# Level two of the first and fifth gate/up products inside PSUM, first pair of a pass plain, last pair between the first down products

## The chip, the cores and the metric

The kernel runs on one core of one Trainium2 chip. Time is device microseconds (us) of one execution. Where two kernels are compared, they ran on the same chip in the same rounds. "Ratio" is the mean time of one kernel's fast runs over the mean of the other's fast runs of the same rounds, so it is not quite the ratio of the medians that are quoted beside it.

## The reference, cut to what matters

```python
# x: 2048 tokens x 1024; w_gate, w_up: 1024 x 3584; w_down: 3584 x 1024
x = x + A(layernorm(x), wqkv, wo)               # linear attention, 32 heads
x = x + B(layernorm(x), w_gate, w_up, w_down)
x = x + A(layernorm(x), wqkv, wo)
x = x + B(layernorm(x), w_gate, w_up, w_down)

def B(x):
    h = (x @ w_gate) * (x @ w_up)               # no nonlinearity
    return h @ w_down
```

## The kernel before

Each layer B is done in two passes of 1024 tokens. A pass has a gate/up stage, in 14 "pairs", and a down stage. A pair is one block of gate columns (A) and the same block of up columns (B). Both stages use a Strassen scheme in Winograd's form: seven products `1` to `7` of half-size blocks instead of eight, with sums of weight blocks and of token blocks made beforehand by VectorE. One product of a pair is 4 matmuls of 512 columns for A and 4 for B.

Some of these products are split a second time ("level two"): gate and up blocks together form a 2 x 2 block product, which becomes seven small products of 2 matmuls with 256 columns each. That is 14 x 256 columns in place of 8 x 512, an eighth less TensorE work. Its price is small sums of tokens and weights, and the assembly of the results. Before, the partial results go from PSUM to SBUF by ScalarE and VectorE and are added in when the product is finished. The orders of work in a pair are strings. `P1A` is product 1 for the gate block, `D2B` finishes product 2 for the up block, and `26` is step 6 of level two of product 2. A prime means that the step belongs to the pair before, `S2+` loads or makes weight sums for the next pair, `R` loads the next weights into a ring of five slots, `T0` and `T1` are places for other work.

```python
L2SETS = {(False, 0): "", (False, 1): "24", (True, 0): "234", (True, 1): "234"}
ORDER0 = "P1A P5A P6A D2A P7A D3B' P1B D4A T0 P6B R0 D3A P7B R1 P5B D4B D2B T1"
ORDER1 = "T0 P1A D3B' 21 P1B 26 P6A 27 P6B S3= D2A 41 D2B P5A 46 P7A 47 P7B D4A P5B R D3A D4B S2+ T1"
ORDER2 = "21 P1A P1B D3A' D3B' 26 S3= P6A T0 27 D2A 41 P6B D2B 46 P7A 31 47 S2+ P7B D4A 36 D4B P5A P5B 37 T1 R"
# first pass: ORDER0; second pass: ORDER1; third and fourth: ORDER2

def st6():                                   # level two, one of its steps
    mm(5, yk, 0, True)
    acp(c5, rc5, yk)                         # ScalarE, PSUM to SBUF
    mm(6, xk, 0, False)
    acp(ss[:, 1], rss[1], xk)
    tt(ss[:, 1], ss[:, 1], c5, ALU.add, ...) # VectorE, in SBUF
# ... cut ...
# last steps of the second layer A: output tiles of 128 tokens, i = 0..15
    y_grp(tok[i], 0, i); y_seed(i + 1); nxt.b2_one(); y_grp(tok[i], 1, i)
    if not first and i == 12:
        for k in range(5):
            stash(3 + k)                     # x tiles to DRAM: their room is wanted
# ... cut ...
def ticks0(u):                               # called at T0 (u even) and T1 (u odd)
    if u % 4 < 2 and not lnp.done():
        lnp.flush_step()                     # one LayerNorm step
    if first and u:
        wd_tick(u)                           # T0: load w_down block, T1: its sums
```

Of the kernel before, what the change touches and what calls it, by code (L numbers as in the profile page):

```python
# [180 lines left out]
def build_kernel(nc, A_x, A_wqkv, A_wo, B_w_gate, B_w_up, B_w_down, out):  # L181
# [5 lines left out]
    SG = 4.0  # L187
# [13 lines left out]
    L2SETS = {(False, 0): "", (False, 1): "24", (True, 0): "234", (True, 1): "234"}  # L201
    ORDER0 = "P1A P5A P6A D2A P7A D3B' P1B D4A T0 P6B R0 D3A P7B R1 P5B D4B D2B T1"
    ORDER1 = "T0 P1A D3B' 21 P1B 26 P6A 27 P6B S3= D2A 41 D2B P5A 46 P7A 47 P7B D4A P5B R D3A D4B S2+ T1"
    ORDER2 = "21 P1A P1B D3A' D3B' 26 S3= P6A T0 27 D2A 41 P6B D2B 46 P7A 31 47 S2+ P7B D4A 36 D4B P5A P5B 37 T1 R"
# [59 lines left out]
    O_TP = {"3": RE, "2": RE + 3072, "4": RB + 28672}  # L264
    O_CP = O_R
    O_SS = [None, O_R + 8192]
    O_C5 = [O_R + 14336, O_R + 15360]
# [25 lines left out]
    KSP = {(q, i): dkey("sp%s%d" % (q, i)) for q in "23" for i in range(2)}  # L293
    KSPW = {(q, i): dkey("spw%s%d" % (q, i)) for q in "23" for i in range(2)}
# [14 lines left out]
    spscr = nc.dram_tensor("sp_scratch", (NJ, 128, 3072), F16, kind="Internal").ap()  # L309
# [5 lines left out]
    with ExitStack() as es:  # L315
# [72 lines left out]
        B_DX = [5, 6, 7, 4]  # L388
# [308 lines left out]
        DPROD = ["1", "2", "7", "4", "6", "5", "3"]  # L697
# [4 lines left out]
        def sp_place(ps_, p, q):  # L702
            sz, so = (2048, 0) if q == "2" else (1024, 2048)
            xp = O_X + (8 * ps_ + 3) * D * 2
            o = {"2": (xp + 4096, RC), "3": (O_R + 12288, xp + 8192)}[q][p % 2]
            return sz, so, o, R(V_SP + 64 * p + so // 64, 32)
# [69 lines left out]

        def tp_ops(pair, prods):
            s0 = pair * 1024
            res = []
            for q in prods:  # L780
                if q == "4":
                    x, base, st_ = T4, O_T + 8192, 1024
                else:
                    s1 = s0 + (512 if q == "3" else 0)
                    x, base, st_ = xblk(1, s1), O_XT + 4 * S * 2 + s1 * 2, S * 2
                o = O_TP[q]
# [8 lines left out]
            return res  # L795
# [54 lines left out]
        def layer_A(lnp, nxt, first):  # L850
# [393 lines left out]
            for i in range(NST):  # L1244
                if na[0] < NST:
                    if i % 3 == 2:
                        norm(tok[na[0]])
                        na[0] += 1
                elif RG["n"] < NR:
                    ring_issue()  # L1250
                nxt.step_t(1)
                nxt.b1_one()
                if i >= 2:
                    nxt.start(i - 2)
                y_grp(tok[i], 0, i)
                y_seed(i + 1)
                nxt.b2_one()
                y_grp(tok[i], 1, i)
                if not first and i == 12:
                    for k in range(5):  # L1260
                        stash(3 + k)
                if not first and i == 14:
                    sp_load(0, 0, "2")
                if nxt.t_next >= 8 and RG["tq"] is None:
                    RG["tq"] = t_ops(0) + tp_ops(0, L2SETS[not first, 0])
                for _ in range(2 if i > 12 else 1):
                    if RG["tq"]:
                        RG["tq"].pop(0)()
# [3 lines left out]
        def layer_B(lnp, nxt, first):  # L1272
# [4 lines left out]
            for f in t_ops(0) + tp_ops(0, L2SETS[not first, 0]) if RG["tq"] is None else RG["tq"]:  # L1277
# [5 lines left out]
            def pair(ps_, p, l2):  # L1283
                xp = O_X + (8 * ps_ + 3) * D * 2
# [4 lines left out]
                o_sp = {q: sp_place(ps_, p, q)[2] for q in "23"}  # L1289
                o_ss = [xp, O_R + 8192]  # L1290
# [40 lines left out]
                def p1(c):  # L1331
                    pe("1", c, X[c], True)
# [18 lines left out]
                def p5(c):  # L1351
                    pe("5", c, Y[c], True)
                    c22(c)

                ORDER = [q for q in "243" if q in l2]

                def l2_of(q):
                    ci = len(ORDER) * p + ORDER.index(q)
                    xk, yk = B_L2[ci % 2], B_L2[(ci + 1) % 2]
                    so = o_ss[ci % 2] if len(ORDER) > 1 else o_ss[0]  # L1360
                    co = O_C5[ci % 2] if len(ORDER) > 1 else O_R + 8192
                    if q == "3":
                        sp, rp = vh(o_sp[q], 1024).rearrange("p (i k c) -> p i k c", i=4, c=128), [R(o_sp[q] + i * 512, 512) for i in range(4)]
                    else:
                        sp = vh(o_sp["2"], 2048).rearrange("p (i b k c) -> p i b k c", i=4, b=2, c=128)[:, :, "42".index(q)]
                        rp = [R(o_sp["2"] + i * 1024, 1024) for i in range(4)]
# [3 lines left out]
                    tp = [(vh(O_TP[q] + i * 1024, 512).rearrange("p (k s) -> p k s", s=256), R(O_TP[q] + i * 1024, 1024)) for i in range(3)]  # L1370
# [5 lines left out]
                          5: ((sp[:, 0], rp[0]), tp[0]), 6: ((sp[:, 1], rp[1]), tp[1]), 7: ((sp[:, 2], rp[2]), b12)}  # L1376

# [5 lines left out]
                    def acp(dst, rd_, bank):  # L1383
                        P.add("act", lambda e: e.activation(dst, psb(bank)[:, 0:256], AF.Copy, scale=SG), prd=[bank], wr=rd_)  # L1384
# [4 lines left out]
                    def st1():  # L1389
                        mm(1, xk, 0, True)  # L1390
                        acp(ss[:, 0], rss[0], xk)

                    def st6():
                        mm(5, yk, 0, True)
                        acp(c5, rc5, yk)
                        mm(6, xk, 0, False)
                        acp(ss[:, 1], rss[1], xk)
                        tt(ss[:, 1], ss[:, 1], c5, ALU.add, rss[1] + rc5, rss[1])

                    def st7():  # L1400
                        mm(7, xk, 0, False)
                        acp(ss[:, 2], rss[2], xk)
# [9 lines left out]

                L = {q: l2_of(q) for q in ORDER}

                def fold_cp(c):
                    s_, r_ = L["3"]["s"](c)
                    t, r = cpb(0, c)
                    tt(s_, s_, t, ALU.add, r_ + r, r_)

                def sums(q, mode):  # L1420
# [3 lines left out]
                    sz, so, o, rv = sp_place(ps_, p, q)  # L1424
# [3 lines left out]
                    for u in units:  # L1428
                        o_ = r_slot(u["n"])[0][0]
                        if q == "2":  # L1430
                            ws.append((vb(o_, 2048).rearrange("p (b i k c) -> p b i k c", b=2, i=2, k=2)[:, :, 0], R(o_, 3072)))
                        else:
                            ws.append((vh(o_ + 6144, 512).rearrange("p (b k c) -> p b k c", b=1, k=2), R(o_ + 6144, 1024)))
# [7 lines left out]
                    dma(spscr[p, :, so:so + sz], vh(o, sz), rv, KSPW[q, p % 2], rd=R(o, 2 * sz))  # L1441

                def fin(q, c):
# [5 lines left out]
                    add = L[q]["s"](c) if q in L else cpb(0, c) if q == "3" else None  # L1449
                    return lambda: mul(c, {"2": "1", "4": "4", "3": "3"}[q], bank, add)  # L1450
                return dict(p1=p1, p5=p5, p6=p6, p7=p7, L=L, fin=fin, fold=fold_cp, sums=sums)

            def gateup(ps_, ticks, l2):
# [11 lines left out]
                def sums(p, q):  # L1465
                    if p < NP and not jit:
                        pairs[p]["sums"](q, "make" if first else "load")

                def fold(p, c):
                    if "3" in l2:  # L1470
                        pairs[p]["fold"](c)
# [3 lines left out]
                def emit(p, tk):  # L1475
                    if tk[-1] == "'":
                        p, tk = p - 1, tk[:-1]
                    if p < 0:
# [6 lines left out]
                    elif tk[0] in "234":  # L1485
                        step(p, tk[0], int(tk[1]))
                        if tk[0] == "3" and tk[1] != "1":
                            fold(p, int(tk[1]) - 6)
                    elif tk[0] == "R":
                        if p or tk == "R1":  # L1490
                            ring_issue()
                        if p and tk == "R":
# [3 lines left out]
                    else:  # L1496
# [5 lines left out]
                        ticks(2 * p + i)  # L1502

                if jit:
                    prep_s(n0)
                    prep_s(n0 + 1)
                for p in range(NP):
                    c = pairs[p]
                    if p == 0:
                        for q in "23":  # L1510
                            if "S%s+" % q in order and not (q == "2" and not first):
                                sums(0, q)
                        for c in range(2 if l2 else 0):
                            emit(0, "P1" + "AB"[c])
                    for tk in order:
                        if p == 0 and l2 and tk[:2] == "P1":
                            continue
                        emit(p, tk)

                def tail():  # L1520
                    for tk in order:
                        if tk[-1] == "'":
                            emit(NP, tk)
                    ring_issue()
                    if "R" in order:
                        ring_issue()
                    for t in range(5):
                        i = 8 * ps_ + 3 + t
# [3 lines left out]
            def down(ps_, ticks, tail):  # L1532
# [18 lines left out]

                for qi, q in enumerate(DPROD):
                    hv, ho = hs[q]
                    wsl = []
                    for hf in range(2):
                        n = ps_ * NPASS + NU + 2 * qi + hf
                        o = r_slot(n)[0][0]
                        wsl.append(((vb if q in "123" else vh)(o, 7 * 512).rearrange("p (j c) -> p j c", c=512), r_slot(n, 0, 7168)))
                    for t in range(4):
                        bank = (B_DX if q in "16" else B_DV)[t]  # L1560
                        start = q in "1275"
                        for hf in range(2):
                            w, rw = wsl[hf]

                            def fn(e, hf=hf, w=w, bank=bank, t=t, start=start, hv=hv):
                                return [e.matmul(psb(bank), hv[:, 7 * hf + k, t * 128:(t + 1) * 128], w[:, k, :],  # L1566
                                                 start=(start and hf == 0 and k == 0), stop=(hf == 1 and k == 6), skip_group_check=True)
                                        for k in range(7)]
# [192 lines left out]
```

## Time and profile before

Median 1472.5 us (1471.8 to 1473.3, 4 runs).

| what | before | where it is read |
|---|---|---|
| TensorE busy | 1451.0 of 1469.6 us, 99% | page, part 1 |
| matmuls of 256 columns (level two) | 1568 = 112 products x 14 | groups |
| 8 matmuls of 512 columns | 1.73 us | chain |
| 10 matmuls of 256 columns | 1.09 us | chain |
| DMA share in the first gate/up pass | 0.98 | windows |

From the page of the kernel before: the span, the busy times with their shares and counts, and the groups of level-one gate/up matmuls (L1307), level-two matmuls (L1380) and down matmuls (L1566). A group's columns are busy time, mean ns of one, and idle time before it.

```profile
span 1469.6 us, 20519 instructions
PE 1451.0 (99%) x7586; PEld 722.1 (49%) x7586; DVE 1149.7 (78%) x2242; ACT 607.5 (41%) x1234; POOL 137.8 (9%) x176
...
L1307 PE MATMUL ps<-arena 128*128 128x512 f16 x2240 | 532.0, 379 | 3.1 <-DVE arena L756 1.1
L1566 PE MATMUL ps<-arena 128*128 128x512 f16 (+1 forms) x1568 | 339.7, 379 | 0.0
L1380 PE MATMUL ps<-arena 128*128 128x256 f16 x1568 | 219.1, 273 | 2.5 <-ACT arena L1384 1.9
```

A busy TensorE alone proves little, since the records of successive matmuls overlap: their mean is 379 ns, but 2240 of them fill only 532.0 us, 238 ns each. The spacing tells it: the chain of waits of the third pass has start, length and what.

```profile
1017.24 1.09 PE ps L1380 x10
1018.33 1.73 PE ps L1307 x8
```

So 512 columns take 216 ns (1.73 us / 8) and 256 take 109 ns (1.09 us / 10). A product at level two then takes 14 x 109 = 1.52 us instead of 1.73 us, a gain of 0.20 us.

The windows view is cut at the first matmul of each part. Its lines are layer A, first pass (gate/up and down together), second pass, second layer A, third pass, fourth pass. The columns are the stretch, its length, and the busy time of each engine in it; then the granted clock, the DMA share and GB/s.

```profile
0.00:240.70 240.70, 234.22 (x1154) 107.75 (x1155) 197.13 (x381) 125.61 (x209) 69.64 (x90) 0.99 0.72 179
240.70:498.20 257.50, 255.25 (x1177) 109.68 (x1176) 178.10 (x356) 67.36 (x114) 2.58 (x6) 1.00 0.86 269
498.20:751.80 253.60, 252.07 (x1345) 128.92 (x1344) 205.79 (x432) 84.45 (x196) 7.94 (x20) 1.00 0.71 238
751.80:972.50 220.70, 217.14 (x1057) 99.29 (x1056) 185.70 (x372) 125.46 (x211) 55.21 (x54) 1.00 0.57 153
972.50:1220.30 247.80, 246.45 (x1429) 138.10 (x1428) 199.36 (x370) 102.89 (x254) 2.42 (x6) 1.00 0.65 217
1220.30:1469.60 249.30, 245.90 (x1429) 138.41 (x1427) 183.64 (x333) 101.74 (x252) 0.00 (x0) 1.00 0.58 200
```

TensorE idles 18.6 us in all, and only 1 to 4 us in each of these parts after the first. It bounds the kernel.

### The profile page before, as it was taken

The page shows a single profiled execution, that of the slowest core. Times are in us where ns is not written, and L with a number is a line of the kernel's source. Part 1 is how long each engine was busy: PE and PEld are TensorE (multiplying, and loading weights), DVE is VectorE, ACT ScalarE, POOL GpSimd, SP SyncE. Part 2 cuts the span into 40 slices and gives each one's busy share as a digit, 9 for nine tenths or more (in the row PEclk, how much of TensorE's full clock was granted, in tenths as well). Part 3 has the DMA queues.
Part 4 walks back from the last instruction along what each step waited for, and adds up shares of the span by engine and source line. Part 5 has one row for each costly group of instructions (what it writes and reads, how often), then busy time and mean ns, then how long its engine had stood idle before and what let it go on. Part 6 is the DMA issues. An engine that isn't in the chain of part 4 may idle for free.

```text
span 1469.6 us, 20519 instructions
## 1 busy us (share of the span) xinstructions
PE 1451.0 (99%) x7586; PEld 722.1 (49%) x7586; DVE 1149.7 (78%) x2242; ACT 607.5 (41%) x1234; POOL 137.8 (9%) x176
## 2 busy tenths in 40 slices
PE   8999999999999999999999999999999999999999
PEld 3444444444444455554444444446666445666544
DVE  6987978777757599986569878799888576888853
ACT  5673356333300244550037823566665004666300
POOL 2213621000000000000010045210000000000000
PEclk9999999999999999999999999999999999999999
DMA  8478967999985668868484167677665756666642
GB/s 258 87 200 225 219 137 177 268 293 296 313 295 189 203 237 255 268 224 286 154 272 129 45 173 158 167 188 244 225 225 184 264 190 220 241 228 228 213 170 94
DMA packets 270163, 310.16 MB, mean 211 GB/s; under 512 B 161904, under 2 KB 212848, under 8 KB 270064
## 3 DMA queue, kind: packets, MB, share of 16 engines
q1 hardware_dynamic: 270064, 308.86, 68.4%
q8 instruction: 60, 0.98, 0.3%
q14 instruction: 39, 0.32, 0.1%
HBM read 230.16 MB, written 69.73 MB: 204 GB/s over the span
## 4 chain that ended last, share of the span: by engine, by line
PE 73%; DVE 13%; DMA 8%; issue 3%; ACT 2%; POOL 1%; SPq 1%; DVEq 0%; ACTq 0%
PE ps L1566 23%; PE ps L1307 21%; PE ps L1380 10%; PE ps L1126 8%; PE ps L907 6%; DMA arena<-in_B_w_down_dram 5%; DVE arena L756 4%; PE ps L878 3%; DVE arena L444 3%; DVE arena L759 2%; DMA arena<-arena 2%; DMA arena<-w_scratch 1%; PE ps L1228 1%; SPq L417 1%; DMA arena<-in_A_wqkv_dram 1%
## 5 line engine op out<-in xcount | busy, mean ns | idle before, releaser
L756 DVE TENSOR_TENSOR arena<-arena 128x512 f16<-128x512 f16 (+8 forms) x1060 | 485.9, 488 | 84.7 <-ACT arena L1384 31.9
L1307 PE MATMUL ps<-arena 128*128 128x512 f16 x2240 | 532.0, 379 | 3.1 <-DVE arena L756 1.1
L759 DVE SCALAR_TENSOR_TENSOR arena<-ps,arena 128x512 f16<-128x512 f32 (+2 forms) x564 | 372.2, 684 | 165.6 <-PE ps L1566 141.8
L1566 PE MATMUL ps<-arena 128*128 128x512 f16 (+1 forms) x1568 | 339.7, 379 | 0.0
L1307 PEld LDWEIGHTS ps<-arena 128*128 128x128 f16 (+1 forms) x2240 | 212.7, 98 | 218.5 <-ACT arena L1312 15.6
L1566 PEld LDWEIGHTS ps<-arena 128*128 128x128 f16 x1568 | 153.3, 98 | 184.0
L1380 PE MATMUL ps<-arena 128*128 128x256 f16 x1568 | 219.1, 273 | 2.5 <-ACT arena L1384 1.9
L1380 PEld LDWEIGHTS ps<-arena 128*128 128x128 f16 (+1 forms) x1568 | 149.1, 98 | 87.5 <-ACT arena L1384 13.3
L1384 ACT ACTIVATE arena<-ps 128x256 f32<-128x256 f32 x448 | 153.4, 383 | 76.6 <-PE ps L1380 73.0
L1333 ACT COPY ps<-ps 128x512 f32<-128x512 f32 x112 | 63.9, 570 | 289.2 <-PE ps L1307 288.1
L1312 ACT ACTIVATE arena<-ps 128x512 f32<-128x512 f32 x224 | 133.7, 597 | 103.3 <-PE ps L1307 92.9
L907 PE MATMUL ps<-arena 128*128 128x512 f16 (+1 forms) x560 | 123.2, 379 | 3.3 <-ACT arena L914 1.2
L1126 PE MATMUL ps<-arena 128*128 128x512 bf16 x512 | 116.1, 379 | 0.0
L1228 PE MATMUL ps<-arena 128*128 128x512 bf16 x512 | 111.0, 379 | 1.3 <-ACT ps L1222 1.3
L444 DVE BATCH_NORM_STATS2 arena<-arena 128x6 f32<-128x512 bf16 x128 | 88.2, 689 | 12.3 <-DMA arena<-in_A_x_dram 7.4
L1009 POOL TENSOR_TENSOR arena<-arena 128x1024 f16<-128x1024 f32 x32 | 77.4, 2419 | 186.3 <-DVE arena L1007 171.9
L878 PE MATMUL ps<-arena 128*128 128x512 bf16 x384 | 86.9, 383 | 3.2 <-ACT arena L548 1.6
L907 PEld LDWEIGHTS ps<-arena 128*128 128x128 f16 x560 | 53.9, 98 | 71.6 <-ACT arena L914 5.4
L447 POOL TENSOR_SCALAR arena<-arena 128x1 f32<-128x1 f32 x64 | 18.9, 295 | 660.7 <-DVE arena L446 660.7
L1228 PEld LDWEIGHTS ps<-arena 128*128 128x128 f16 x512 | 50.0, 98 | 62.0 <-ACT ps L1222 2.3
L1126 PEld LDWEIGHTS ps<-arena 128*128 128x128 f16 x512 | 49.3, 98 | 55.7
L609 ACT ACTIVATE arena<-ps 128x512 bf16<-128x512 f32 x88 | 53.0, 602 | 39.8 <-PE ps L878 27.8
(53 smaller groups left out, 625.6 us busy)
## 6 DMA issues: line engine op xcount, KB each, us to landing
arena<-w_scratch SPq DMA_DIRECT2D x84, 896.0 KB, 6.0
arena<-t_scratch SPq DMA_DIRECT2D x32, 896.0 KB, 5.7
arena<-in_B_w_down_dram SPq DMA_DIRECT2D x24, 896.0 KB, 6.9
w_scratch<-arena SPq DMA_DIRECT2D x28, 512.0 KB, 7.6
arena<-sp_scratch SPq DMA_DIRECT2D x28, 512.0 KB, 3.6
arena<-w_scratch SPq DMA_DIRECT2D x28, 384.0 KB, 5.6
x_scratch<-arena SPq DMA_DIRECT2D x36, 256.0 KB, 6.9
arena<-x_scratch SPq DMA_DIRECT2D x36, 256.0 KB, 6.3
```

Of the source, the lines that this page charges most:

```text
L444: P.add("dve", (lambda h: lambda e: e.bn_stats(st[j][:, 6 * h:6 * h + 6], x_res[:, i, (D // 2) * h:(D // 2) * (h + 1)]))(h), rd=r_x(i, (D ...
L756: P.add("dve", lambda e: e.tensor_tensor(out=out, in0=a, in1=b, op=op), rd=rd, wr=wr, prd=prd)
L759: P.add("dve", lambda e: e.scalar_tensor_tensor(out=out, in0=a, scalar=sc, in1=b, op0=ALU.mult, op1=op1), rd=rd, wr=wr, prd=prd)
L878: return [e.matmul(psb(bank), xnT[:, k, i * 128:(i + 1) * 128], t[:, k, h * 512:(h + 1) * 512], start=(k == 0), stop=(k == KT - 1)) for k ...
L907: P.add("pe", lambda e: [e.matmul(psb(bank), a[0][:, k, :], b[0][:, k, :], start=(q in (1, 5) and k == 0), stop=(k == 3), skip_group_check ...
L1126: return [e.matmul(psb(bank), xrt[t][:, jj * 128:(jj + 1) * 128], pk[:, h, t, :], start=(t == tok[0]), stop=(t == tok[NST - 1])) for t in ts]
L1228: return [e.matmul(psb(bank), xnT[:, g, i * 128:(i + 1) * 128], wp[:, g, dh * 512:(dh + 1) * 512], start=(dh == 0 and g == 0), stop=(g == ...
L1307: P.add("pe", lambda e: [e.matmul(psb(bank), w[:, k, :], x[:, k, :], start=(start and k == 0), stop=(k == 3), skip_group_check=True) for k ...
L1312: P.add("act", lambda e: e.activation(t, psb(bank), AF.Copy, scale=SG), prd=[bank], wr=r)
L1380: P.add("pe", lambda e: [e.matmul(psb(bank)[:, 256 * half:256 * half + 256], w[:, k, :], xx[:, k, :], start=(start and k == 0), stop=(k == ...
L1384: P.add("act", lambda e: e.activation(dst, psb(bank)[:, 0:256], AF.Copy, scale=SG), prd=[bank], wr=rd_)
L1566: return [e.matmul(psb(bank), hv[:, 7 * hf + k, t * 128:(t + 1) * 128], w[:, k, :], start=(start and hf == 0 and k == 0), stop=(hf == 1 an ...
```

## The change

Its intent: do level two for products 1 and 5, and no longer for 3 (nor, in the second pass, for 2). Counting one pair in each of the four passes, that makes 12 products at level two instead of 8. Products 1 and 5 are assembled inside PSUM (ScalarE copies and VectorE additions from one bank into another), so that less SBUF room is needed for them. The first pair of each pass stays plain, so that the token sums need not be ready at the start. Much of a pair's end moves into the next pair (the primes), and for the last pair of a pass between the first down products. The first down products are gathered in PSUM too, in a changed order of products, and in the second pass the LayerNorm work moves from the pairs to the down stage. Because more of `x` is overwritten by buffers, eight tiles of it instead of five are stashed. Cut to the core:

```diff
-    L2SETS = {(False, 0): "", (False, 1): "24", (True, 0): "234", (True, 1): "234"}
+    L2SETS = {(False, 0): "5", (False, 1): "154", (True, 0): "1245", (True, 1): "1245"}
+    ORDER0 = "D3A' P5B' R0 51 D4B' T0 P1A D3B' 56 P1B P6A R0 T1 D2A P6B P7A P5A 57 S5+ D2B P7B D4A"
+    ORDER1 = "D4A' P5B' 11 D3A' 51 16 D4B' D2B' T1 R0 P1A 17 D3B' P6A 56 S5+ T0 P1B 41 D2A 57 R0 P6B S2+ 46 P7A P5A 47 P7B"
+    ORDER2 = "11 57' D2B' P7B' 16 T0 P5A' 21 D4B' P1A 17 S2+ D3A' P5B' 26 R0 P6A D2A S5+ 41 27 P1B D3B' 46 51 T1 P7A 47 P6B 56 D4A R0"
 ... (the old orders go) ...
-                if not first and i == 12:
-                    for k in range(5):
-                        stash(3 + k)
+                if not first and i == 9:
+                    for k in range(8):
+                        stash(k)
 ...
+    def put(c, h):        # half a bank to half a bank
+        P.add("act", lambda e: e.copy(half(c, h), U), prd=[xk], pwr=[dst[c]])
+    def put5(c):
+        P.add("dve", lambda e: e.tensor_tensor(out=half(c, 1), in0=U, in1=c5, op=ALU.add), prd=[xk], rd=rc5, pwr=[dst[c]])
     def st6():
-        mm(5, yk, 0, True)
-        acp(c5, rc5, yk)
-        mm(6, xk, 0, False)
-        acp(ss[:, 1], rss[1], xk)
+        mm(6, xk, 1, False)
+        if dst:           # products 1 and 5
+            put5(0)
+            return
+        acp(ss[:, 1], rss[1], U, SG)
 ...
+    pre = ("P1A", "P1B") + (("P5A", "P5B") if l2 else ())     # first pair, plain, at the start
+    L = {q: l2_of(q) for q in ORDER} if p else {}
 ...
+    for part, th in enumerate(((0, 0), (1, 0), (0, 1))):      # first down products
+        grp(*th)
+        tail(part + 1)                                        # a third of the last pair's rest
 ...
-                if u % 4 < 2 and not lnp.done():
+                if u % 2 == 0 and not lnp.done():             # LayerNorm step at T0 of every pair
```

## The prediction

> **What bounds it now.** The page gives TensorE 1451.0 of 1469.6 us busy (99%), so TensorE work bounds the kernel. By stretches (windows view): the four gate/up passes take 172.9, 168.1, 165.2 and 160.9 us, the four down stages about 85.5 each at 100% TensorE. The chain of waits shows a matmul every 216 ns at 512 columns (8 in 1.73 us) and every 109 ns at 256 (10 in 1.09 us). [...]
>
> **What the change does.** A plain product of a pair is 8 matmuls of 512 columns (1.73 us); at level two it is 14 of 256 (1.52 us): 0.20 us less. Before, level two is done 0+2+3+3 times over 14 pairs = 112 times (1568/14, groups view); after, 1+3+4+4 times over 13 pairs (first pair plain) = 156. 44 more x 0.20 us = 9 us of TensorE time, nearly all on the critical path. Running the last pair between the first down products, and starting passes plain, only moves TensorE work, but should remove the short idles at the starts of passes (1.07 us waiting for VectorE at 241.7; 0.5 at 501; 1.0 over three at 975-991): about 2 us more. Down stages: 392 matmuls each as before, no change. Stashing and reloading 8 tiles instead of 5 is hidden (DMA share 0.65).
>
> **What takes it back.**
> - First gate/up pass: DMA share is already 0.98, SyncE issues without pause, and the chain of waits runs through the w_down load (about 8.4 us), its VectorE preparation and back, once per pair of 12.35 us. TensorE alone would need 12.1. VectorE gets about 2 us more per pair (four sums at 286 ns, two PSUM additions at about 420), on top of 10, and the load is now issued behind a ring load that waits for the pair before. I expect no gain here: 0, between -2 and +8.
> - Second pass: VectorE is busy 157.4 of 168.1 us. The LayerNorm work (about 17 us) leaves for the down stage; larger sums and the PSUM additions come in, about 11.3 us per pair against 11.5 of TensorE. TensorE now waits on these additions within 1 to 2 us, where before only ScalarE copies stood there. Gain about 3.
> - Passes three and four: VectorE per pair about 10.0 of 11.3 us, ScalarE 14 instead of 12 level-two copies of 383 ns; pair from 11.49 to about 11.3. Gain 2 to 2.5 each less stalls, with the idles removed about 4 together.
>
> Sum: about 7 us less: **1465 us, 8 in 10 between 1457 and 1477.** Faster by over 2%: 0.02; within 2%: 0.95; slower by over 2%: 0.03.
>
> **What would show it.** 2184 matmuls of 256 columns (156 x 14). TensorE busy near 1442. Windows: passes three and four about 2 us shorter each once the moved last pair is counted; first pass not shorter, with VectorE waiting for DMA and TensorE idle before its matmuls; down stages without idle. The waits view would show TensorE (or its weight loads) waiting on the new PSUM additions.
>
> **What would make it wrong.** If the reordered first pass runs at TensorE's pace, 1458 is reached. If its load-prepare loop binds, its pairs go to 13 us or more and the kernel is slower than before. If additions queue behind VectorE work, each may cost tenths of a us, four times per pair: up to 20 us.

The sum is that of the passes: 0 for the first, about 3 for the second and about 4 for the third and fourth together, 7 us less. The 216 and 109 ns are read from the chain of waits.

## The result, and the profile after

1476.8 us median (1473.7 to 1480.0, 4 runs) against 1472.5 of before: ratio 1.0029, interval 1.0005 to 1.0053. That is within 2%, as forecast, but 7 us fewer were predicted and 4 us more came. The runs also spread over 6 us, where those of before spread over 1.4.

The same lines of the page, after (L1310 level-one gate/up, L1596 down, L1391 level two):

```profile
span 1473.8 us, 21078 instructions
PE 1442.5 (98%) x7850; PEld 755.0 (51%) x7850; DVE 1126.3 (76%) x2248; ACT 655.9 (45%) x1354; POOL 138.9 (9%) x176
...
L1310 PE MATMUL ps<-arena 128*128 128x512 f16 x1888 | 459.2, 380 | 5.6 <-DVE arena L760 5.1
L1596 PE MATMUL ps<-arena 128*128 128x512 f16 (+1 forms) x1568 | 340.9, 379 | 0.0
L1391 PE MATMUL ps<-arena 128*128 128x256 f16 x2184 | 289.8, 273 | 8.7 <-ACT arena L1395 4.8
```

The TensorE work fell as computed: 2184 = 156 x 14 level-two matmuls, busy 8.5 us less (predicted 9, to 1442). But TensorE's idle time rose from 18.6 to 31.3 us, by 12.7, and 12.7 - 8.5 = 4.2 us is just the difference of the spans. The windows view, cut in the same places, says where:

```profile
0.00:241.40 241.40, 233.38 (x1154) 107.42 (x1155) 197.63 (x382) 126.16 (x209) 68.42 (x90) 1.00 0.73 179
241.40:501.10 259.70, 254.17 (x1255) 122.39 (x1254) 188.79 (x417) 80.33 (x157) 2.58 (x6) 0.99 0.83 259
501.10:753.50 252.40, 247.49 (x1411) 136.86 (x1410) 200.48 (x416) 100.49 (x233) 10.98 (x20) 1.00 0.77 253
753.50:978.80 225.30, 219.08 (x1058) 99.59 (x1057) 184.35 (x370) 124.63 (x210) 54.49 (x54) 0.99 0.57 150
978.80:1224.40 245.60, 244.15 (x1490) 144.40 (x1489) 182.00 (x341) 112.82 (x274) 2.42 (x6) 1.00 0.72 237
1224.40:1473.80 249.40, 244.19 (x1489) 144.31 (x1487) 173.05 (x325) 111.49 (x272) 0.00 (x0) 1.00 0.63 216
```

| part | before | after | difference | saving due (0.20 us x products) |
|---|---|---|---|---|
| layer A | 240.7 | 241.4 | +0.7 | 0 |
| first pass | 257.5 | 259.7 | +2.2 | -2.6 (13 - 0) |
| second pass | 253.6 | 252.4 | -1.2 | -2.2 (39 - 28) |
| second layer A | 220.7 | 225.3 | +4.6 | 0 |
| third pass | 247.8 | 245.6 | -2.2 | -2.0 (52 - 42) |
| fourth pass | 249.3 | 249.4 | +0.1 | -2.0 (52 - 42) |

Only the third pass got its saving. Against what was due, the four passes and the two layers A together fall about 13 us short. Most is missing in the first pass (4.8 us) and in the second layer A (4.6 us), where the change moves the stashes, makes them eight, and takes out one load and some sums of tokens. The waits of TensorE (total us, times, longest) name the new pauses:

```profile
PE ps L1310 <- DVE arena L760: 5.1, 5, 2.6
PE ps L1391 <- ACT arena L1395: 4.8, 7, 1.2
PE ps L1232 <- ACT ps L1226: 4.0, 2, 2.4
PE ps L1391 <- DMA arena<-sp_scratch: 1.8, 1, 1.8
```

The first line is all in the first pass (the longest of its five pauses is 2.63 us, before 254.4), the second in the second pass (seven pauses from 578 to 653), the third in the second layer A (2.36 us of it before 968.4), the fourth in the fourth pass (before 1234.1). Each has its own cause.

*First pass.* The timelines of TensorE and of VectorE around its longest pause:

```profile
254.35 1.15 PE L1310 MATMUL ps<-arena 128*128 128x512 f16 x4 [2.63 <-DVE arena L760]
250.72 2.98 DVE L757 TENSOR_TENSOR arena<-arena 128x512 f16<-128x512 bf16 x8
```

The step L760 that TensorE needs runs at 253.61, behind eight weight sums (L757) and, before these, a LayerNorm step of about 2 us. VectorE has no pause from 241 to 258 us: it is behind with its work.

*Second layer A.* The timelines of SyncE's issues, of ScalarE and of TensorE around the pause (start, length, what, idle before and what ended it):

```profile
955.38 6.03 SPq L416 DMA_DIRECT2D x_scratch<-arena  x8
961.44 7.11 SPq L531 DMA_TRANSPOSE arena<-arena  x3
...
966.06 1.24 ACT L460 ACTIVATE arena<-arena 128x1024 f16<-128x1024 bf16 x1 [6.37 <-DMA arena<-arena]
967.20 0.56 ACT L1240 CAST arena<-ps 128x512 bf16<-128x512 f32 x1
967.80 0.59 ACT L1226 CAST ps<-arena 128x512 f32<-128x512 bf16 x1
...
968.44 1.84 PE L1232 MATMUL ps<-arena 128*128 128x512 bf16 x4 [2.36 <-ACT ps L1226]
```

SyncE spends 6.0 us on issuing the eight stashes. The next transpose, which empties one of two LayerNorm buffers, is issued only then. ScalarE waits 6.37 us for that buffer, and the small copy L1226 that seeds TensorE's next bank stands behind it. And the four matmuls after the pause take 1.84 us, where four took 1.03 us elsewhere. The granted clock in that stretch, and after the pause in the first pass (windows view, first and second line; the clock is the third number from the end):

```profile
254.30:258.60 4.30, 4.25 (x14) 1.92 (x15) 3.62 (x9) 0.66 (x2) 0.00 (x0) 0.60 1.12 306
968.40:971.80 3.40, 3.36 (x9) 1.16 (x10) 3.33 (x7) 2.37 (x4) 0.79 (x2) 0.52 0.73 140
```

Cut more finely, the view gives 0.50 from 255.15 to 258.55 and from 968.53 to 971.94, and 1.00 in the 3.4 us after each. So for 3.4 us after each of these two pauses the clock is at half speed, which by an estimate (half of 3.4) costs another 1.7 us each time. So two pauses of 5.0 us together cost about 8.4.

*Second pass.* The chain of waits of one pair (pieces "issue" of 0.02 us left out):

```profile
581.61 6.92 DMA arena<-w_scratch
588.56 0.30 DVE arena L757
588.88 0.69 DVE arena L757 x3
589.58 0.35 DVE ps L1404
589.95 0.36 ACT ps L1401
...
591.16 0.39 PE ps L1391 x2
```

The pause of TensorE here is put down to a ScalarE copy, but it begins with a ring load. VectorE waits for it to make the next pair's weight sums (L757), and the addition inside PSUM (L1404), which TensorE needs, stands behind those sums. The timeline shows the same: VectorE stood idle for 2.17 us until the sums began at 588.56, and L1404 ran only behind them, at 589.50.

*Fourth pass.* The chain of waits has the load of weight sums for the second pair, issued only behind the last stores of the pass before, and it ends when the pause ends:

```profile
1225.80 8.27 DMA arena<-sp_scratch
```

### The profile page after: what moved, and what is told of

Its sections match the earlier page's. It is cut to its first block, busy times and chain, and to the rows that moved or that the text cites. A ratio compares the mean times of both kernels' runs of the same rounds, so it can differ in the third digit from the quotient of the medians.

```text
span 1473.8 us, 21078 instructions
## 1 busy us (share of the span) xinstructions
PE 1442.5 (98%) x7850; PEld 755.0 (51%) x7850; DVE 1126.3 (76%) x2248; ACT 655.9 (45%) x1354; POOL 138.9 (9%) x176
## 4 chain that ended last, share of the span: by engine, by line
PE 74%; DVE 11%; DMA 9%; issue 2%; ACT 2%; POOL 1%; SPq 1%; DVEq 0%; ACTq 0%; POOLq 0%
PE ps L1596 23%; PE ps L1310 21%; PE ps L1391 14%; PE ps L1130 6%; PE ps L911 6%; DMA arena<-w_scratch 3%; DVE arena L757 3%; DMA arena<-arena 3%; PE ps L882 3%; DVE arena L443 2%; DMA arena<-in_B_w_down_dram 2%; DVE arena L1007 1%; SPq L416 1%; DVE arena L1004 1%; PE ps L1232 1%
## 5 line engine op out<-in xcount | busy, mean ns | idle before, releaser
L757 DVE TENSOR_TENSOR arena<-arena 128x512 f16<-128x512 f16 (+10 forms) x951 | 432.4, 480 | 96.1 <-ACT arena L1395 32.4
L760 DVE SCALAR_TENSOR_TENSOR arena<-ps,arena 128x512 f16<-128x512 f32 (+2 forms) x497 | 334.3, 686 | 175.1 <-PE ps L1596 151.3
L1310 PE MATMUL ps<-arena 128*128 128x512 f16 x1888 | 459.2, 380 | 5.6 <-DVE arena L760 5.1
L1596 PE MATMUL ps<-arena 128*128 128x512 f16 (+1 forms) x1568 | 340.9, 379 | 0.0
L1391 PE MATMUL ps<-arena 128*128 128x256 f16 x2184 | 289.8, 273 | 8.7 <-ACT arena L1395 4.8
L1310 PEld LDWEIGHTS ps<-arena 128*128 128x128 f16 (+1 forms) x1888 | 183.5, 98 | 170.3 <-DVE arena L760 9.3
L1391 PEld LDWEIGHTS ps<-arena 128*128 128x128 f16 (+1 forms) x2184 | 211.3, 98 | 102.6 <-ACT arena L1395 14.0
L1596 PEld LDWEIGHTS ps<-arena 128*128 128x128 f16 x1568 | 153.4, 98 | 183.1
L1395 ACT ACTIVATE arena<-ps 128x256 f32<-128x256 f32 x351 | 125.3, 385 | 24.4 <-PE ps L1391 20.1
L1401 ACT COPY ps<-ps 128x256 f32<-128x256 f32 x182 | 65.8, 362 | 135.3 <-DVE ps L1404 73.9
L911 PEld LDWEIGHTS ps<-arena 128*128 128x128 f16 x560 | 53.9, 98 | 71.6 <-ACT arena L918 5.4
L1232 PEld LDWEIGHTS ps<-arena 128*128 128x128 f16 x512 | 50.2, 99 | 66.4 <-ACT ps L1226 5.4
L1404 DVE TENSOR_TENSOR ps<-ps,arena 128x256 f32<-128x256 f32 x182 | 77.8, 428 | 2.6 <-PE ps L1391 2.6
```

Of the source, the lines that this page charges most:

```text
L757: P.add("dve", lambda e: e.tensor_tensor(out=out, in0=a, in1=b, op=op), rd=rd, wr=wr, prd=prd)
L760: P.add("dve", lambda e: e.scalar_tensor_tensor(out=out, in0=a, scalar=sc, in1=b, op0=ALU.mult, op1=op1), rd=rd, wr=wr, prd=prd)
L911: P.add("pe", lambda e: [e.matmul(psb(bank), a[0][:, k, :], b[0][:, k, :], start=(q in (1, 5) and k == 0), stop=(k == 3), skip_group_check ...
L1232: return [e.matmul(psb(bank), xnT[:, g, i * 128:(i + 1) * 128], wp[:, g, dh * 512:(dh + 1) * 512], start=(dh == 0 and g == 0), stop=(g == ...
L1310: P.add("pe", lambda e: [e.matmul(psb(bank), w[:, k, :], x[:, k, :], start=(start and k == 0), stop=(k == 3), skip_group_check=True) for k ...
L1391: P.add("pe", lambda e: [e.matmul(psb(bank)[:, 256 * half:256 * half + 256], w[:, k, :], xx[:, k, :], start=(start and k == 0), stop=(k == ...
```

## The experiments

Theory: the saving is real, and it was given back where DMA issues and VectorE work were put in a worse order, with the two pauses of 2.63 and 2.36 us paid again through the clock (about 1.7 us each). Main rival: TensorE now waits for copies and additions inside PSUM within 1 to 2 us, and these waits are the price of doing level two there. Single-edit runs are judged by their part of the windows view, since the whole time also carries the other, varying losses.

### Stash one tile per step

```diff
-                if not first and i == 9:
-                    for k in range(8):
-                        stash(k)
+                if not first and i >= 8:
+                    stash(i - 8)
```

> After, with one change: in the second layer A the eight tiles of x are stashed one per step in steps 8 to 15, instead of all eight in step 9. Theory (a burst of DMA issues delays the transposes, ScalarE waits for a buffer, TensorE idles 2.4 us and its clock is then halved for 3.4 us): the gap of 2.36 us near 968 and the half-clock stretch there vanish, TensorE stretch of this layer 225 -> about 221 us, kernel about 4 us shorter than the changed kernel (about 1472). Rival (the loss is the PSUM additions that TensorE now waits for, not DMA order): under 1 us of change.

Measured: 1472.0 us (1468.5 to 1475.4, 4 runs) against 1474.8 of before, ratio 0.998 (0.996 to 1.000). The second layer A took 220.9 us, as long as before the change (220.7), and the pause at 968 and its half-clock stretch were gone (granted clock 1.00 over this layer, 0.99 before the edit). The theory holds: 4.4 us of this layer's 4.6 were DMA order and the half-clock stretch that followed from it. All kept traces of the changed code agree: the five without a burst at step 9 took 220.9 to 222.2 us here, the six with it 223.4 to 225.5. Of these six, the three in which the clock halved took 225.1 to 225.5 and the three in which it did not 223.4 to 223.8: about the 1.7 us that a half-clock stretch costs. The half-clock stretch of the first pass remained, and another one appeared in the second pass after a pause of 2.45 us (granted clock 0.99 over each of the two passes). The single run of this kernel whose granted clock was 1.0 was also its shortest, 1468.5; the others (0.998) took 1470.7 to 1475.4.

### No LayerNorm step at the first tick

```diff
-                if u % 2 == 0 and not lnp.done():
+                if u and u % 2 == 0 and not lnp.done():
```

> After, with one change: no LayerNorm step at the first tick of the first and third gate/up pass (about 2.2 us of VectorE work there is done a pair later). Theory (the first pair of the first pass is short of TensorE work that doesn't need VectorE, because its first and fifth products were hoisted, so VectorE's backlog stops TensorE for 2.63 us and halves its clock for 3.4 us): the gap near 254 falls under 1 us, the half-clock stretch there goes, first pass about 4 us shorter, kernel about 3 to 4 us shorter than the changed kernel. Rival (backlog is set by the weight preparation, or half-clock stretches come at random): under 1 us, or the half-clock stretch stays.

Measured: 1474.7 us (1471.7 to 1479.2, 4 runs) against 1474.8, ratio 1.000. The pause at 254 fell from 2.63 to 0.64 us, with no half-clock stretch after it (granted clock 1.00 over the pass), and the first pass took 257.3 instead of 259.7 us, less than the 4 us I expected. In the third pass, however, a new pause of 1.45 us came where the step was put off: the edit was right for the first pass and, by this pause, wrong for the third. The later runs make it in the first pass alone.

### Ring load earlier, sums later

```diff
-    ORDER1 = "D4A' P5B' 11 D3A' 51 16 D4B' D2B' T1 R0 P1A 17 D3B' P6A 56 S5+ T0 P1B 41 D2A 57 R0 P6B S2+ 46 ..."
+    ORDER1 = "D4A' P5B' 11 D3A' R0 51 16 D4B' D2B' T1 P1A 17 D3B' P6A 56 T0 P1B 41 D2A 57 R0 P6B S5+ S2+ 46 ..."
```

> After, with one change in the second gate/up pass: the first ring load of a pair is issued after its D3A' instead of three products later, and the sums of the fifth product are made after P6B instead of after 56. Theory (VectorE's sums of the next pair wait for a ring load that lands 6 to 7 us after its issue, and the PSUM additions queue behind them): TensorE's idle in this pass falls from 4.7 to about 1 us, seven gaps of 0.2 to 1.2 us go, kernel about 3.5 us shorter than the changed kernel. Rival (TensorE waits for the additions by themselves, VectorE being full): the gaps stay, under 1 us.

Measured: 1472.9 us (1469.7 to 1473.7, 4 runs) against 1474.8, ratio 0.998 (0.997 to 1.000). The second pass took 250.7 instead of 252.4 us. The waits on that copy became twelve of at most 0.2 us:

```profile
PE ps L1391 <- ACT arena L1395: 2.4, 12, 0.2
```

So the rival is right about 2.4 us at most in this pass, an even 0.2 us per pair, and the theory about the rest; TensorE's idle time fell from 4.9 to 2.7 us, not to the 1 I expected. The other traces make the case firmer than this one pair does: with the old order of the pass, seven traces have 3.8 to 8.3 us of waits on this copy (up to 3.1 us each) and the pass took 250.9 to 256.2 us; with the new order, four have 2.4 or 2.5 us (at most 0.2 each) and took 250.6 to 251.0. The edit has two halves that were not tried apart.

### Early load of weight sums

```diff
+                if q == "5" and t == 3 and not first:       # in the down stage of the third pass
+                    sp_load(1, 1, "2")
-                    if p < NP:
+                    if p < NP and (first or (ps_, p, q) != (1, 1, "2")):
```

> After, with one change: the load of the weight sums for the second pair of the last gate/up pass is issued during the down stage before, instead of behind its last stores. Theory: the gap of 1.81 us near 1234 goes, kernel about 1.8 us shorter. Rival: the load was late because the DMA engines were full, so that the gap moves elsewhere: no change.

Measured: 1473.8 us (1470.9 to 1476.3, 4 runs) against 1474.8, ratio 0.999. The pause at 1234 was gone and the fourth pass took 247.5 instead of 249.4 us: nearly its whole saving. The load had stood behind the last stores of the pass before in SyncE's queue. The two later runs that have this edit and keep the last pair where it was agree to 0.1 us, and seven traces without it took 248.8 to 249.9.

### Control, all four edits, and level two taken out of the first pass

The changed kernel itself, on the occasion of the next three:

> The changed kernel again, as the control on this chip: ratio to before near 1.003, runs spread over some 5 us, the shorter runs those without half-clock stretches (granted clock 1.0), the longer ones 0.997 to 0.998.

Measured: 1472.3 us (1471.8 to 1473.9, 5 runs) against 1470.9 of before, ratio 1.001 (1.000 to 1.002). Here the clock halved only once after the start, following a pause of 3.13 us in the second pass (granted clock 0.99 over it), and not after pauses of 2.62 and 2.49 us (1.00 over the first pass and the second layer A). So whether a pause is charged by the clock changes from run to run (the last section has the count), and that is one source of the changed kernel's spread. It is not the only one: on the first occasion the runs do stand in the order of their granted clocks (1473.7 us at 1.0, 1475.5 and 1478.0 at 0.998, 1480.0 at 0.997), here they do not, and one run of the LayerNorm experiment took 1479.2 us at 1.0. A second source is the ring load of the second pass: without the ring edit that pass alone differs by 5 us between traces (250.9 to 256.2), with it by 0.4. No trace was kept of the slowest runs, so that what made them slow stays open.

All four edits, the LayerNorm step left out only in the first pass:

> After with the four edits together (stash one tile per step; no LayerNorm step at the first tick of the first pass alone; earlier ring load and later sums in the second pass; early load of the weight sums). Theory (the level-two saving of 8.5 us is real and was given back by waits behind DMA and VectorE queues, doubled where they halve the clock): 10 to 12 us shorter than the changed kernel, ratio to before about 0.994 to 0.996. Rival (waits only move on): under 4 us shorter than the changed kernel, ratio about 1.0 or above.

Measured: 1463.0 us (1462.0 to 1463.6, 5 runs) against 1470.9 of before and 1472.3 of the changed kernel: ratio 0.994 (0.993 to 0.996). It beats both, by about 8 and 9 us (differences of the medians; I had expected 10 to 12 against the changed kernel), and its spread is 1.6 us. Its windows from the first pass on:

```profile
241.40:496.90 255.50, 252.89 (x1256) 121.76 (x1255) 188.74 (x417) 80.22 (x157) 2.37 (x6) 1.00 0.84 264
496.90:747.50 250.60, 248.15 (x1412) 135.33 (x1411) 199.22 (x416) 102.13 (x233) 10.98 (x20) 1.00 0.75 254
747.50:968.50 221.00, 217.18 (x1058) 99.24 (x1057) 184.25 (x369) 124.82 (x210) 54.38 (x54) 1.00 0.58 152
968.50:1214.10 245.60, 244.07 (x1489) 144.39 (x1488) 182.09 (x341) 112.87 (x274) 2.42 (x6) 1.00 0.72 241
1214.10:1461.60 247.50, 244.09 (x1489) 144.42 (x1487) 173.09 (x325) 111.53 (x272) 0.00 (x0) 1.00 0.62 215
```

Against before, the four passes gain 2.0, 3.0, 2.2 and 1.8 us, together 9.0 us, the full saving of 44 x 0.20; the second layer A is within 0.3 us. After the start no pause over 2 us is left and the clock stays at 1.00. That the sum fits so exactly is partly luck, since single parts differ by more between traces (the first pass of the LayerNorm experiment, with the same code there, took 257.3 us, not 255.5); the 8 us of the medians are the firmer number.

Level two out of the first pass, its old order put back:

```diff
-    L2SETS = {(False, 0): "5", ...
+    L2SETS = {(False, 0): "", ...
+    ORDER0 = "P1A P5A P6A D2A P7A D3B' P1B D4A T0 P6B R0 D3A P7B R1 P5B D4B D2B T1"
```

> After with level two taken out of the first pass and its order of before put back. Theory (the first pass is bound by DMA and VectorE together, so that level two there gains nothing): first gate/up and down stage together 257 to 258 us as in before, against 259.7 in the changed kernel, so 2 us shorter, though it has 2.7 us more TensorE work. Rival (only the start-up gap of 2.63 us and its half-clock stretch hurt the first pass): the rest of the pass is 2.7 us longer, so that the pass comes to no less than 258.

Measured: 1472.5 us (1470.8 to 1477.7, 4 runs) against 1470.9, ratio 1.002. Its first pass took 258.0 us, at the edge between the two expectations, so I set it against the other version:

> The three other edits (stash, ring, early load) with level two taken out of the first pass. If level two gains nothing in the first pass this equals the version with all four edits within 1 us; if it does gain there once the start-up gap is gone, this is up to 2.7 us longer.

Measured: 1464.5 us (1462.8 to 1465.6, 5 runs), ratio 0.995 (0.994 to 0.997). The first pass took 257.2 us, against 255.5 with level two and the start-up pause repaired. The traces don't settle it: with level two and the same repaired code the LayerNorm experiment took 257.3, and without level two three traces, that of the kernel before among them, took 257.2 to 258.0. The medians do point to a gain, of 1.5 us, but the ranges of the five runs each overlap (1462.0 to 1463.6 against 1462.8 to 1465.6). So level two probably gains in the first pass, and my claim that DMA and VectorE forbid a gain there is weakened rather than refuted. What hurt the changed kernel's first pass was the start, where VectorE had more queued than TensorE could cover: taking one LayerNorm step away ended the long pause. That hoisting products 1 and 5 of the first pair, and the early ticks, brought it about is argued and was not tried apart.

### Where the burst stands

```diff
-                if not first and i == 9:
+                if not first and i == 12:
```

> After with the eight stashes of the second layer A in one burst at step 12, where before has its five. Theory (it is the size of the burst, 8 DMA issues in about 6 us, in front of the transposes): a gap before matmuls of this layer remains, 1.5 to 2.5 us, only later. Rival (it is the place, step 9 instead of 12): no gap over 0.6 us after the one near 950 that before has too, and the layer takes about 221 us.

One look: the second layer A took 220.9 us. Its pauses over 0.6 us were 1.04 us near 789 and 1.39 us near 952, and before has both (1.04 and 1.31). By this one execution the rival was right: eight stashes in a burst do no harm at step 12. It is the place that matters, step 9, where the LayerNorm transposes behind the burst are still needed soon.

### Last pair not between the down products

```diff
-  lo, hi = (0, nd2) if part == 0 else (nd2 + n * (part - 1), min(nd2 + n * part, len(late)))
+  lo, hi = (0, len(late)) if part == 0 else (0, 0)
```

> The version with all four edits, but with the last pair of each pass run before the first down product instead of between the down products. Theory of the change (down products give ScalarE and VectorE time for the additions of the last pair): idle of 0.3 to 1 us before the down stage of each pass, kernel 1 to 4 us longer than with the last pair in between (ratio to before 0.995 to 0.997). Rival (it only moves TensorE work): the same within 0.7 us, ratio about 0.994.

Measured: 1471.9 us (1471.5 to 1473.8, 4 runs) against 1469.9 of before, ratio 1.001 (0.999 to 1.002), where all four edits gave 0.994: 9 to 10 us lost, more than twice my upper figure. Its passes took 259.4, 251.0, 248.3 and 250.5 us, that is 3.9, 0.4, 2.7 and 3.0 us more than with the last pair in between (the first and the third also differ by up to 2 us between traces of the same code). The waits show TensorE stopped at the end of the passes, by 2.3 us in the first (with a half-clock stretch after it; granted clock 0.99 over the pass) and by 1.30 and 1.36 us, one for each of the two lines below, in the third and again in the fourth:

```profile
PE ps L1309 <- DVE arena L760: 7.1, 7, 2.3
PE ps L1390 <- ACT arena L1314: 2.6, 2, 1.3
```

With so much of a pair pushed into the next one, the last pair leaves a string of steps that wait for one another. With the down products in between, these pauses are gone: independent work fills the waits.

## Why the prediction was wrong

7 us less were forecast and 4 more came, a difference of 11 us by the parts of the two traces: 4.6 in the second layer A, 2.2 in the first pass, 1.8 in the second, 1.9 in the third and fourth together, and 0.7 in the first layer A, whose code is the same.

- **TensorE saving.** Right. Predicted 9 us and busy near 1442; the profile says 8.5 and 1442.5, and the repaired version collects 9.0 us over the four passes. The match of 1442.5 is closer than it deserves: two half-clock stretches are in it, and the repaired kernel, without them, is busy for 1440.3 us.
- **"Stashing and reloading 8 tiles instead of 5 is hidden (DMA share 0.65)."** This step failed worst. I judged a burst by a mean DMA share, and looked at the stages where it is reloaded rather than at the one where it is issued. It cost 4.6 us in the second layer A, a part of the kernel that I had left out of the sum. The number of tiles was not what failed, since eight at step 12 did no harm: what counted here was which small transfer stood behind the burst in SyncE's queue, and who waited for it.
- **Passes starting plain "should remove the short idles".** Wrong for the first pass. The idle of 1.07 us at its start became 0.42, but one of 2.63 us came a pair later, behind a backlog of VectorE. I had costed VectorE per pair, not for the first pair. That the four hoisted products left too little TensorE work there is my reading; no run shows it apart. In the second pass the 0.5 us did go; in the third the 1.0 us became 1.3.
- **First pass: no gain, between -2 and +8.** The measured +2.2 lies inside, but the reason was wrong: not the w_down loop, which the chain of waits shows before the change, but the start. That it lies inside is luck. Repaired, the pass gained 2.0 us in one trace and 0.2 in another.
- **Second pass: gain about 3.** 1.2 measured in this trace; others of the same code there range from a gain of 2.7 to a loss of 2.6. The step "larger sums and the PSUM additions come in" counted VectorE's work, about 11.3 us per pair, and not its wait for the ring load, which was issued too late by about 2 us. The prediction did name the risk ("if additions queue behind VectorE work"), but not what would make them queue. With the load earlier and the sums later, the gain is 3.0.
- **Passes three and four: about 4 together.** 2.1 measured; the missing 1.8 us is one load behind the last stores of the pass before.
- **"Only moves TensorE work."** Wrong in size: putting the last pair between the down products carries 9 to 10 us of the repaired version. It is no gain over before, which left one or two steps over at the end of a pass, but without it the new orders would not pay.
- **What I had no term for.** After 9 of the 14 pauses between 2.3 and 3.1 us the clock was at half speed for 3.4 us, about 1.7 us more each. Two such charges make about 3.4 of the 13 us by which the changed kernel fell short. They appear as busy time and so are not among the 12.7 us of added idle time.

## What to carry to other kernels

When TensorE is busy 99% of the time, as here, a saving in its work can be given back in the queues in front of it: after such a change, list the new pauses one by one with their releasers, and follow each back to the first instruction that was late, which here was a DMA issue or a VectorE backlog, and in two of the four cases (both put down to ScalarE) not the engine named. Judge a burst of transfers by what stands behind it in the issuing queue, not by the mean DMA share. Cost the first and the last pair of a pipelined loop separately, because the sum per pair missed both here.

## What the traces showed of the clock and of a burst of DMA issues

- In the traces of all these kernels, after the first 12 us and before the last matmul, I counted 14 gaps of TensorE of 2.27 to 3.13 us, and after 9 of them the clock records show half speed for 3.4 us (about 1.7 us lost each); the gaps up to 2.02 us were never followed by one, and none came without such a gap. In the changed kernel's first trace, those of 2.63 and 2.36 us were, those of 1.81 and 1.60 us were not. The same gap of 2.62 to 2.63 us at the start of the first pass was charged in three runs and spared in three; what set these apart is left open here. (In the first 12 us half speed also came after shorter gaps: in the kernel before the clock was 0.50 from 8.5 to 11.8 us, and the longest gap between matmuls up to there was 0.94 us.)
- Eight stores of 256 KB held SyncE for 6.0 us, where a single one of them takes from 0.43 us, and the transpose behind them came so much later. One of the eight took 2.17 us, and no view shows why; the same burst at step 12 (the run with one execution) took 4.74 us.
